# A transformer block with sliding attention and a token-mixing MLP: another hand-written issue order, with fillings in front of the first transposes

## The chip, the cores and the metric

The kernel runs on one core of one Trainium2 chip. The core has five engines that work side by side: PE (TensorE, matmuls), DVE (VectorE), ACT (ScalarE), POOL (GpSimd) and SP (SyncE, which here only issues DMAs). The metric is the device time of one launch in microseconds. Lower is better.

## The reference, cut

```python
mod = (silu(c) @ w_mod).reshape(1, 6, 1, 512)            # c: 1 x 512, w_mod: 512 x 3072
sa, ca, ga, sb, cb, gb = (mod[:, i] for i in range(6))
h = layernorm(x) * (1 + ca) + sa                          # x: 1 x 2048 x 512, bf16
x = x + ga * A(h)
h = layernorm(x) * (1 + cb) + sb
x = x + gb * B(h)
# A: qkv = h @ wqkv (512 x 1536); 32 heads of 16; each token attends to itself and the 7 tokens
#    at distances 2, 4, ..., 14 before it (softmax over 8); then @ wo (512 x 512)
# B: h = layernorm(h); u = gelu(w1^T h + b1) (w1: 2048 x 1792, over the tokens);
#    y = w2^T u + b2 (w2: 1792 x 2048)
```

A mixes neighbouring tokens. B mixes all tokens: every column of `w1` needs all 2048 rows of h.

## The kernel before, in words

**Tiles and chunks.** The 2048 tokens are 16 tiles of 128. They go through A in five chunks (numbered 0 to 4) of 2, 4, 4, 4 and 2 tiles, which begin at tiles 0, 2, 6, 10 and 14. In names a single digit after the kind of step is a chunk, and where tiles are meant the number runs from 0 to 15.

**First norm and transposition.** For each tile `ln1s` takes the statistics (on DVE one instruction; on ACT two passes with accumulation), `ln1v` gathers them, and `rstd1_`, `rste1_` and `nb1_` give one over the deviation and the shift for a chunk. `n1_` normalizes a tile. Chunks 0 and 1 are transposed on PE (`tr`) and copied out of PSUM with a scaling by `a1col`, which is 1 + ca as a column (`hT0_0` to `hT1_3`). Chunks 2 to 4 are transposed by DMAs that SP issues (`xt6` to `xt15`); for them `wqkv` itself is scaled by `a1col` (`wsc{t}_{kt}`; t is 0 for queries, 1 for keys, 2 for values). `a1col` comes from `modcols1`, 16 matmuls of one column of silu(c) with a part of `w_mod`. silu(c) comes from `cps`, a matmul on the loaded c (`ld_c`), an exponential on ACT and three instructions on DVE.

**Attention.** `qkv{chunk}_{t}{j}` are the products with `wqkv`, `ev...` the evictions that follow them (ACT or DVE). `qk` is a large elementwise product of queries and shifted keys on DVE; `red` sums it over a head's 16 numbers with matmuls on PE. `max`, `sub`, `exp`, `esum`, `rcp`, `rcq` and `smB` are the softmax. `a2_{chunk}_{0..3}` are four DMAs that spread the probabilities over the partitions, and `vd{chunk}_{0..3}` four DMAs that make shifted copies of the values (pool `vd`, five places). `pv` is the large product of both on DVE; it needs all four `a2_` of its chunk and its own `vd`. `pvacc` sums it on PE, `oev` evicts, `wo{tile}` multiplies by `wo` and adds the residual (with one matmul by the identity where ACT evicts, in the eviction where DVE does: `x1_{tile}`). `wo` has been scaled by ga (`woq_s`), which with the other rows of the modulation comes from `modrow`, `mrows` and the small loads `ld_row0` to `ld_row3`.

**Second and third norm, MLP.** `ln2*`, `n2_`, `aff`, `afb`, `ln3*` and `h3_` give h of B. `mlp1_{sweep}_{column}_{tile}` are partial products of the first MLP matrix over the tiles that are ready, in three sweeps; `park` and `padd` keep and add the partial sums in SBUF, `gelu` closes a column. `mlp2_{tile}`, `fin` and `st_out` are the second matrix, its bias and residual, and the stores.

**What sets the order.** All of the above is built as a graph of named steps. A table of names, `ORDER` (lines 180 to 235), gives the order in which they are issued, and nothing else plans: `schedule()` (line 87) walks the table, gives each step that needs one the place of its pool that came free first (6 PSUM banks `ps`, 4 product buffers `big`, 5 `vd`), and each engine runs its own steps in that order. A suffix chooses another of a step's forms: `:a` ACT, `:d` DVE, `:p` POOL, `:s` leaves it out, and `:q` splits each matmul into four strips of 32 output columns:

```python
def mm(out, lhsT, rhs, **kw):
    if not G.quad:
        return nc.tensor.matmul(out, lhsT=lhsT, rhs=rhs, **kw)
    for j in range(0, P, 32):
        nc.tensor.matmul(out[j:j + 32], lhsT=lhsT[:, j:j + 32], rhs=rhs, tile_position=(0, j), **kw)
```

Matmuls of `red`, `pvacc` and `modrow` have the strip form always. So the table says how often PE changes between the full form and the strip form.

**Fillings.** `WARM` gives the number of matmuls (512 columns of the identity, result not used) in the steps `warm0` to `warm7`. Before, it is `(12, 2, 2, 2, 2, 2, 2, 2)`. `warm0` is made to follow `cps` and to lie ahead of `modcols1` by a key (`wmA1`, lines 538, 553 and 556); `warm2` to `warm7` carry `:s` in the table, and `warm1` stands at its end.

All instructions are issued through one wrapper (`_EngProxy`), so every row of the profile says line 131; the steps are told apart by what they read and write: `xx` is x, `h` the normalized tiles, `hT` their transposes, `wst` a ring of weight places, `q_sb`, `k_f`, `v_sb` queries, keys and values, `lsb` the probabilities, `a2sb` the spread ones, `vD` the shifted values, `big` the products, `psS` and `psL` PSUM, `gT` the rows of the MLP.

Of the kernel before, what the change touches and what calls it, by code (L numbers as in the profile page):

```python
# [42 lines left out]
class _Graph:  # L43
# [7 lines left out]
    def add(self, eng, dur, fn, **kw):  # L51
        return self.add_any([(eng, dur, fn)], **kw)
# [138 lines left out]
nb1_3 a2_0_0 ln1s15:a a2_0_2 qkv2_00 qk1_2 qkv2_10 n1_13:p red1_0 ev2_00 red1_1 ev2_10 red1_2 red1_3 ln1v15 a2_0_1
ev1_23 qkv2_13:q qk2_0 ev1_21 max1 modrow qkv1_20:q sub1:q ln1s14:a a2_0_3 pv0_0 wsc2_1:a halo_v1:a qkv1_22:q mrows
vd0_3 vd0_1 vd0_2 ld_wo1 ev2_13 pv0_3 pvacc0_0 n1_10 exp1 ev1_20 ld_row0 qkv2_02:q pv0_1 pv0_2 warm3:s ld_wo2 esum1:q
rcp1 ev1_22 rcq1 smB1 qkv2_03 ev2_03 pvacc0_1 pvacc0_2 xt10 wsc2_0:a pvacc0_3 ev2_02 oev0_2 qkv2_01:q vd1_3 qkv2_12
oev0_0 ev2_01 ln1v14 qkv2_11 ev2_12 rstd1_4 qkv2_23:q n1_11 vd1_1 n1_12 a2_1_2 qkv2_22:q a2_1_3 qk2_3 woq_s rste1_4
wo1:q wo0:q ev2_11 a2_1_0 a2_1_1 vd1_2 x1_1 red2_0 qk2_2 nb1_4 qk2_1 ev2_22 qkv2_20 x1_0 ev2_23 ln2m0 biascols pv1_3
n1_14 xt13 xt12 ln2q0 ln2q1 n1_15 qkv2_21 red2_1 red2_2 ln2w0 red2_3 xt11 rstd2_0 pv1_1 ev2_21 rste2_0 qkv3_10:q
ev3_10 qkv3_02:q ev3_02 qkv3_00:q ev2_20 ev3_00 nb2_0 n2_1 n2_0 qkv3_11 max2 qkv3_01 ev3_01 sub2 pvacc1_1 oev1_1
halo_v2 ld_row2 vd1_0 pvacc1_3 pv1_2 qkv3_12:q ld_row1 exp2 aff0 ev3_12 qkv3_13:q halo_v3:a ev3_11 pv1_0 esum2
pvacc1_2 rcp2 oev1_3 oev1_2 afb0 pvacc1_0 oev1_0 rcq2 xt14 ld_w1_0_0 ld_w1_0_512 vd2_2 qkv3_03:q qk3_1 smB2 ln3s0:a  # L200
# [10 lines left out]
mlp1_0_7_0:q pv3_2 pvacc3_0 mlp1_0_5_2:q oev3_0 esum4:q nb2_6 n2_7 mlp1_0_6_2:q warm7:s rcp4 pv3_1 n2_6 park0_5 pv3_3
n2_9 pvacc3_2 n2_8 aff6 oev3_2 mlp1_0_7_2:q rcq4 pvacc3_1 oev3_1 mlp1_0_8_2:q smB4 ld_w1_0_1152 mlp1_0_10_0:q
ld_w1_0_1408 pvacc3_3 vd4_2 mlp1_0_10_2 vd4_0 warm2:s park0_6 oev3_3 wo11 afb6 x1_11:d a2_4_3 ln3s8 ln3v8 ln3s9:a wo10
wo13 ln3s6 vd4_1 ln3v9 ln3v6 ln3s7 wo12 x1_10 ln2m10 ln3v7 mlp1_0_9_0 ln2q11 x1_12:d mlp1_0_9_2 ln2q10 a2_4_0 ln2w10
rstd3_6 rste3_6 nb3_6 a2_4_2 h3_6:d h3_7:d mlp1_0_12_0 mlp1_0_12_2 h3_8:d rstd2_10 h3_9 mlp1_0_7_6 mlp1_0_8_6 ln2q12
# [23 lines left out]
def kernel(  # L239
# [72 lines left out]
    mask = T([32, NW, PAD], BF, "mask")  # L312
# [716 lines left out]
```

## Time and profile before

| | |
|---|---|
| runs | 198.03, 198.26, 198.43 us; median 198.26 |
| span of the profiled execution | 196.8 us, first to last instruction |
| own time of that execution | not recorded beside the span; the median lies 1.46 us above it |
| PE busy | 185.2 us (94%) |
| DVE busy | 156.6 us (80%) |
| ACT busy | 124.9 us (63%) |
| POOL busy | 19.9 us (10%) |
| DMA queue of SP | 34.05 MB, 63.2% of the time of 16 engines |

A row of the timeline is: start in us from the first instruction, duration, engine, line, operation, tile out <- tiles in, shape, and in brackets how long the engine had waited and for whom. Rows of equal instructions in a row are put together as xN, and the duration is then that of the whole run. PEld is the loading of weights into PE, which runs beside its matmuls; a `q` behind an engine (SPq, ACTq) is its issue of a DMA. In a table of windows stand the stretch, its length, and the busy time of each engine in it with the number of its instructions, then the clock that PE was granted (1.00 is full), the busy share of the DMA engines and GB/s. In a table of groups stand the count, the busy time in us, the mean of one in ns, and the idle time of the engine just before, with its releaser. A row of DMA issues has the count, the size of one and the median time from issue to landing.

### The profile page before, as it was taken

To read this page: it belongs to the slowest core of one execution; us is meant where nothing else is said; L and a number is where in the kernel's file an instruction comes from. 1 tells how busy PE (TensorE), PEld (TensorE's weight loads), DVE (VectorE), ACT (ScalarE), POOL (GpSimd) and SP (SyncE) were. 2 spreads that over 40 slices of the span, in tenths; PEclk is the share of its full clock that TensorE was granted. 3 is DMA by queue.
4 is the path that set the end of the run, shared out by engine and by line. 5 is a ranking of instruction groups with operands and counts; after the bars stand their busy time and mean duration, and the time that the engine had idled before them with its cause. 6 is when DMAs were issued, how large, how long until landed. Compare 5 with 4: busy or idle time off the path is not lost.

```text
span 196.8 us, 4628 instructions
## 1 busy us (share of the span) xinstructions
PE 185.2 (94%) x1850; PEld 95.5 (48%) x1867; DVE 156.6 (80%) x244; ACT 124.9 (63%) x293; POOL 19.9 (10%) x38
## 2 busy tenths in 40 slices
PE   0699999999999999899999999999999999999994
PEld 0369554654444467244544454444444444444453
DVE  2888999999999999999999999965841633453664
ACT  6877999998999999999797889812760000000000
POOL 5123006320000005030000031200000000000000
PEclk9999999999999999999999999999999999999999
DMA  5998478778899732969674768888939293001112
GB/s 169 312 366 248 115 165 256 235 216 238 165 193 317 252 131 80 312 167 249 199 200 136 159 176 180 197 250 170 336 65 309 82 257 102 30 27 53 53 53 82
DMA packets 55369, 35.95 MB, mean 183 GB/s; under 512 B 24628, under 2 KB 52788, under 8 KB 55348
## 3 DMA queue, kind: packets, MB, share of 16 engines
q1 hardware_dynamic: 53468, 34.05, 63.2%
q10 hardware_dynamic: 1880, 1.61, 2.5%
q8 instruction: 14, 0.23, 0.5%
q14 instruction: 7, 0.06, 0.1%
HBM read 22.03 MB, written 2.10 MB: 123 GB/s over the span
## 4 chain that ended last, share of the span: by engine, by line
PE 73%; DVE 13%; ACT 5%; issue 3%; DMA 2%; SPq 1%; POOL 0%; DVEq 0%; ACTq 0%
PE psS L131 71%; DVE big L131 9%; DVE h L131 2%; PE psL L131 2%; ACT junk L131 1%; SPq L131 1%; DMA vD<-v_sb 1%; ACT xx L131 1%; DMA xx<-in_A_x_dram 1%; DVE m L131 1%; ACT o_sb L131 1%; ACT lsb L131 0%; DVE mv L131 0%; POOL h L131 0%; ACT v_sb L131 0%
## 5 line engine op out<-in xcount | busy, mean ns | idle before, releaser
L131 PEld LDWEIGHTS <-wst 128*128 128x128 bf16 (+1 forms) x566 | 35.5, 100 | 31.9 <-issue 1.3
L131 PE MATMUL psS<-h,wst 128*32 128x512 bf16 (+1 forms) x400 | 50.5, 379 | 0.4 <-issue 0.3
L131 DVE TENSOR_TENSOR big<-q_sb,k_f 128x4096 bf16<-128x4096 bf16 (+1 forms) x20 | 36.4, 1857 | 0.5 <-ACT k_f L131 0.5
L131 DVE TENSOR_TENSOR big<-a2sb,vD 128x4096 bf16<-128x4096 bf16 (+1 forms) x20 | 36.6, 1858 | 0.0
L131 DVE SCALAR_TENSOR_TENSOR h<-psS,bcol,rows_bc 128x512 f32<-128x512 f32 (+2 forms) x18 | 12.4, 690 | 24.2 <-PE psS L131 24.0
L131 PE MATMUL psS<-hT,w_qkv 128*32 128x512 bf16 (+3 forms) x414 | 28.7, 337 | 0.8 <-ACT v_sb L131 0.4
L131 PEld LDWEIGHTS <-w_qkv 128*32 128x32 bf16 (+1 forms) x462 | 19.9, 108 | 16.4 <-issue 2.7
L131 PE MATMUL psS<-gT,big 128*128 128x512 bf16 x109 | 24.3, 379 | 0.2
L131 POOL TENSOR_SCALAR h<-xx,rs,nb 128x512 bf16<-128x512 bf16 x6 | 10.6, 1777 | 84.2 <-DVE nb L131 84.2
L131 PEld LDWEIGHTS <-big 128*128 128x128 bf16 x144 | 12.0, 98 | 13.7 <-issue 0.5
L131 ACT ACTIVATE junk<-xx 128x512 bf16<-128x512 bf16 x28 | 17.7, 631 | 1.3 <-DVE xx L131 0.3
L131 ACT ACTIVATE h<-xx,nb,rs 128x512 bf16<-128x512 bf16 x22 | 17.2, 818 | 0.4 <-DVE nb L131 0.4
L131 PE MATMUL psS<-woq,o_sb 128*32 128x512 bf16 (+1 forms) x123 | 15.8, 380 | 0.4 <-ACT o_sb L131 0.4
L131 ACT ACTIVATE gT<-psS,bcol 128x512 bf16<-128x512 f32 x14 | 8.8, 686 | 10.6 <-DVE psS L131 10.6
L131 DVE TENSOR_TENSOR psS<-psS,gT 128x512 f32<-128x512 f32 x14 | 9.2, 695 | 6.3 <-PE psS L131 6.3
L131 DVE TENSOR_TENSOR h<-h,xx 128x512 bf16<-128x512 f32 (+2 forms) x18 | 11.4, 633 | 0.7
L131 ACT ACTIVATE q_sb<-psS,qvb 128x512 bf16<-128x512 f32 (+1 forms) x20 | 11.6, 603 | 0.3 <-PE psS L131 0.2
L131 PEld LDWEIGHTS <-group 128*32 128x32 bf16 x288 | 7.0, 96 | 9.8 <-issue 4.0
L131 PE MATMUL psS<-hT,wst 128*128 128x256 bf16 (+2 forms) x74 | 11.3, 333 | 0.1
L131 ACT ACTIVATE v_sb<-psS,qvb 128x512 bf16<-128x512 f32 (+1 forms) x20 | 11.2, 607 | 0.0
L131 DVE TENSOR_TENSOR h<-h,rows_bc 128x1024 bf16<-128x1024 bf16 (+2 forms) x14 | 10.5, 759 | 0.0
L131 ACT ACTIVATE k_f<-psS 128x512 bf16<-128x512 f32 x16 | 9.7, 606 | 1.1 <-PE psS L131 1.1
(90 smaller groups left out, 223.3 us busy)
## 6 DMA issues: line engine op xcount, KB each, us to landing
vD<-v_sb SPq DMA_DIRECT2D x12, 524.5 KB, 4.8
big<-in_B_w_dram SPq DMA_DIRECT2D x4, 896.0 KB, 7.5
vD<-v_sb SPq DMA_DIRECT2D x8, 268.5 KB, 3.1
wst<-in_B_w_dram SPq DMA_DIRECT2D x3, 640.0 KB, 5.4
xx<-in_A_x_dram SPq DMA_DIRECT2D x7, 256.0 KB, 5.6
wst<-in_B_w_dram SPq DMA_DIRECT2D x2, 800.0 KB, 4.7
gT<-in_w_mod_dram SPq DMA_DIRECT2D x3, 512.0 KB, 5.4
wst<-in_B_w_dram SPq DMA_DIRECT2D x2, 768.0 KB, 5.6
```

What stands on the lines that cost most here:

```text
L131: r = fn(*a, **k)
```

## The change

Five edits. All but two are in the table.

1. `WARM` becomes `(2, 8, 1, 3, 8, 5, 2, 1)`, and all eight steps are now issued. On PE: `warm0` to `warm3` (14 matmuls), `cps`, `warm4` and `warm5` (13), the transposes of chunk 0, `warm6` (2), `modcols1`. `warm7` (1) stands in front of `wo7`. The key `wmA1` is gone.
2. The load of c (`ld_c`, issued by ACT) moves from the front of the table to behind `rste1_0` on ACT; `ident` is the first work of POOL, and the zero halos (`halo0`) come behind the constants.
3. SP's queue has another order. At the front: tiles 0 and 1 of x, then the pairs 4-5, 2-3, 8-9, 6-7, both parts of `w_mod`, the query weights (`ld_wqkv0`), **the pair 10-11 of x (chunk 3's first)**, the key weights (`ld_wqkv1`), the value weights, the pairs 12-13 and 14-15. Later: the four `a2_0` are preceded by `vd0_3` alone; `ld_wo2`, `ld_wo3`, `xt10`, `ld_wo0`, `ld_wo1`, `ld_b1`, `ld_row0`, `vd1_1`, `xt11`, `a2_1_3`, `xt12`, `a2_1_1`, `a2_1_2`, `a2_1_0`, `xt13`, `ld_row2`, `vd1_0`, `vd1_3`, `vd1_2`. Before, in that place: three of the four `ld_wo` earlier, `vd1_3`, `vd1_1`, the four `a2_1`, `vd1_2`, `xt13`, `xt12`, `xt11`, `ld_row2`, `vd1_0`.
4. Other engines. From ACT to DVE 17 steps: the evictions `ev0_00`, `ev0_02` and `ev1_22`, `n1_1`, `n1_3`, `n1_8`, `n2_14`, `h3_5`, `h3_9`, `x1_10`, and statistics of seven tiles. From ACT to POOL 11: `n1_7`, `n1_9`, `n1_14`, `n2_3`, `h3_10`, `h3_15`, `halo_v4`, and the weight scalings `wsc1_0`, `wsc1_1`, `wsc2_0`, `wsc2_2`. From DVE to ACT 20: `hT0_2`, `hT1_0`, `hT1_2`, `n1_2`, `n1_4`, `n1_5`, `wsc0_0`, five `h3_` and eight statistics. From POOL to ACT five (`n1_13`, `n2_5`, `n2_15`, `wsc1_2`, `halo_v2`), from POOL to DVE three (`n1_0`, `wsc0_2`, `h3_11`), from DVE to POOL one (`h3_12`). `nb1_0` is left out (its tiles are normalized on DVE), `nb3_12` and `nb3_14` are issued. Of the stores eight go from ACT to SP and two from SP to ACT.
5. Fewer steps carry `:q`: PE's matmul and weight-load instructions fall from 3736 to 3496. The order of steps on every engine is another, the kinds of work and their sum the same; in the MLP other columns go into the first sweeps' early and late pieces, and the last pieces of the last tile end in the order 0, 1, 2 (before 0, 2, 1).

```diff
-halo0 ident ld_c act_table cps silu_exp ld_x1 ld_x0 ln1s0 ln1v0 ln1s1:a ln1v1 rstd1_0 rste1_0 ld_x_2_8 ld_x_1_2 nb1_0
-consts ln1s9 silu_dve n1_1 n1_0:p tr0_0 ln1s8 ld_x_1_4 ln1s4:a ld_x_2_6 ln1s3:a warm0 ln1s5 ln1s7 ld_wmod1 ln1v5
-ld_wmod0 modcols1 modcols0 ln1v9 ln1v8 ln1v4 ln1s2 ln1v2 ld_wqkv0 ln1v7 ln1v3 ln1s6 ln1v6 rstd1_1 rste1_1 nb1_1 n1_4:d
-rstd1_2 rste1_2 n1_2:d n1_5:d nb1_2 ld_wqkv1 n1_3 n1_7 n1_6:d a1col hT0_2:d n1_9 tr1_2 tr1_0 hT1_1 wsc0_1:p hT0_1:d
-sab hT0_0:d ld_x_3_12 hT0_3:d hT1_3:d qvb0 qvb_cp0 qkv0_00 warm6:s wsc1_3:a hT1_2:d qkv0_02 ev0_00 ld_wqkv2 qkv0_10
-qkv0_12 ld_b2 ev0_10 ld_x_4_14 wsc1_2:p qkv0_20 wsc0_0 qvb1 ld_x_3_10 wsc0_3:p hT1_0:d ev0_02 wsc2_2:a ln1s13 ln1s12
...
+ld_x0 ident act_table ln1s0 consts ld_x1 ln1s1 ln1v1 ln1v0 rstd1_0 warm0 rste1_0 ld_x_1_4 ln1s5 ld_c warm1 ld_x_1_2
+nb1_0:s ld_x_2_8 warm2 ln1s4 ln1v5 ln1s3 n1_0:d ln1v3 n1_1:d ln1s2:a ln1v4 ln1v2 ld_x_2_6 ln1s8 warm3 cps rstd1_1
+rste1_1 silu_exp nb1_1 ln1s6:a warm4 ld_wmod1 warm5 ln1s9 halo0 silu_dve ln1v9 tr0_0 n1_4 warm6 ln1s7 ld_wmod0
+modcols1 ld_wqkv0 a1col n1_2 wsc0_1:p n1_5 wsc0_3:p ln1v6 modcols0 ln1v8 ln1v7 ld_x_3_10 rstd1_2 rste1_2 hT0_3:d hT0_2
+ld_wqkv1 n1_3:d hT0_1:d hT0_0:d tr1_0 nb1_2 tr1_2 sab hT1_0 ln1s10 hT1_2 ld_wqkv2 ld_x_3_12 qvb0 ln1s11:a n1_9:p
+hT1_3:d wsc0_0:a qkv0_00 hT1_1 qkv0_02 qvb_cp0 qkv0_10 n1_8:d qkv0_12 wsc0_2 ld_x_4_14 qkv0_22 ld_wmod2 ev0_10 ev0_12
+ev0_02:d qkv0_20 ld_wmod3 n1_6:d xt6 qkv1_11 wsc2_3:a n1_7:p qvb1 ld_wmod4 ev0_00:d qk0_0 qk0_1 red0_0 qkv1_01:q
...
+ev2_01 n1_11 ld_b1 ev2_11 pvacc0_1 ev2_10 n1_12 qkv2_03:q ev2_03 pvacc0_3 ld_row0 n1_13 vd1_1 oev0_2 smB1 qkv2_00
+oev0_0 xt11 a2_1_3 qkv2_20 xt12 qkv2_22 qk2_2 a2_1_1 ev2_00 qkv2_13 ev2_13 qk2_1 woq_s qk2_0 qk2_3 wo1 x1_1 ln2q1
+ev2_21 wo0 red2_0 a2_1_2 x1_0 ln2m0 ln2q0 qkv2_23:q a2_1_0 red2_1 ev2_23 ev2_20 pv1_1 halo_v2:a xt13 ld_row2 vd1_0
+ln2w0 rstd2_0 rste2_0 red2_2 red2_3 ev2_22 qkv3_03 max2 ev3_03 qkv3_11 qkv3_10 vd1_3 sub2 qkv3_01 vd1_2 ev3_10 nb2_0
...
-    WARM=(12, 2, 2, 2, 2, 2, 2, 2),
+    WARM=(2, 8, 1, 3, 8, 5, 2, 1),
...
-        if w_ == 0:
-            f_warm0, s_w0 = f_warm, s_w
-            continue
...
-    add("pe", 0.216 * WARM[0], f_warm0, after=[G.ops[-1]], alloc=s_w0, frees=s_w0, writes=["wmA1"], name="warm0")
...
-    add("pe", 0.42, lambda: f_cols(1), reads=["sc", ("wmodA", 1), "wmA1"], writes=["wmA1"], alloc=s_m[1], name="modcols1")
+    add("pe", 0.42, lambda: f_cols(1), reads=["sc", ("wmodA", 1)], alloc=s_m[1], name="modcols1")
```

More of the change, by code (lines that the diff above doesn't have):

```diff
@@ L191 @@
[L191 to L200, printed above, removed]
@@ L211 @@
[L211 to L215, printed above, removed]
@@ new lines @@
+a2_0_3 rstd1_4 qk1_3 ev1_22:d rste1_4 nb1_4 halo_v1:a n1_14:p vd0_0 rstd1_3 vd0_2 vd0_1 rste1_3 red1_3 wsc1_2:a
+wsc1_3:a nb1_3 max1 pv0_3 qkv2_02 ev1_20 qkv2_01 ld_wo2 pv0_0 ld_wo3 n1_10 n1_15 ev2_02 sub1 exp1 ev1_21 qkv2_12
+modrow ev2_12 pvacc0_0 mrows esum1:q qkv2_21:q pv0_2 pv0_1 rcp1 pvacc0_2 qkv2_11:q rcq1 xt10 ld_wo0 qkv2_10:q ld_wo1
+ev2_01 n1_11 ld_b1 ev2_11 pvacc0_1 ev2_10 n1_12 qkv2_03:q ev2_03 pvacc0_3 ld_row0 n1_13 vd1_1 oev0_2 smB1 qkv2_00
+oev0_0 xt11 a2_1_3 qkv2_20 xt12 qkv2_22 qk2_2 a2_1_1 ev2_00 qkv2_13 ev2_13 qk2_1 woq_s qk2_0 qk2_3 wo1 x1_1 ln2q1
@@ new lines @@
+pv3_3 park0_4 park0_5 n2_7 esum4:q ld_w1_0_1408 rcp4 n2_8 aff6 rcq4 park0_6 mlp1_0_10_0:q vd4_0 oev3_1 mlp1_0_9_0:q
+vd4_2 mlp1_0_9_2:q afb6 pvacc3_0 mlp1_0_10_2:q pvacc3_3 oev3_0 oev3_3 smB4 a2_4_0 ln3s7:a ln3s6 mlp1_0_8_2 a2_4_2 wo12
+a2_4_3 wo11 x1_12:d wo13 x1_11:d ln3s9 a2_4_1 vd4_3 wo10 ln3s8:a x1_10:d ln2m10 mlp1_0_11_0 mlp1_0_11_2 mlp1_0_12_0
+ln2q11 mlp1_0_12_2 ln2q10 ln3v7 ln3v9 ln3v6 ln3v8 x1_13:d ln2m12 mlp1_0_7_0 rstd3_6 rste3_6 mlp1_0_7_2 nb3_6 h3_7:d
+h3_8:d h3_6 ln2q12 ln2w10 h3_9:d mlp1_0_7_6 vd4_1 rstd2_10 rste2_10 ln2q13 mlp1_0_8_6 pv4_2 mlp1_0_9_6 nb2_10 pv4_1
```

70 lines of the change are left out of this document (36 added, 34 removed).

## The prediction

> **What bounds the kernel now.** I read the page first, then the busy time of four stretches, then the timeline of each engine around the places that the change touches.
>
> ```profile
> span 196.8 us, 4628 instructions
> PE 185.2 (94%) x1850; PEld 95.5 (48%) x1867; DVE 156.6 (80%) x244; ACT 124.9 (63%) x293; POOL 19.9 (10%) x38
> ```
>
> ```profile
> 12.33:42.00 29.67, 29.30 (x400) 19.49 (x405) 28.45 (x38) 27.46 (x60) 8.64 (x6) 1.00 0.73 206
> 42.00:102.00 60.00, 58.29 (x885) 29.96 (x887) 59.87 (x60) 57.25 (x140) 4.71 (x4) 1.00 0.78 211
> 102.00:126.00 24.00, 23.68 (x220) 11.04 (x219) 23.51 (x64) 20.39 (x58) 3.30 (x4) 1.00 0.73 185
> 126.00:191.00 65.00, 64.68 (x299) 29.65 (x304) 33.64 (x51) 10.78 (x16) 0.00 (x0) 1.00 0.50 139
> ```
>
> The columns after the length are PE, PEld, DVE, ACT and POOL. PE's 94% tempts one to call the kernel PE-bound and every filled PE gap a gain. The stretches say otherwise. From 42 to 102 DVE is busy 59.87 of 60.00 us, PE 58.29. From 126 on DVE is half idle and PE is full: 299 matmuls in 65 us, 0.217 us each. Where one bound hands over to the other is seen at 102:
>
> ```profile
> 97.35 4.49 DVE L131 TENSOR_TENSOR big<-a2sb,vD 128x4096 bf16<-128x4096 bf16 x2
> 101.89 0.62 PE L131 MATMUL psS<-big,group 128*32 128x512 bf16 x8
> ```
>
> DVE ends the last two value products of chunk 3 at 97.35 + 4.49 = 101.84, and PE starts their sum (pvacc3_3) at 101.89. PE stands there because DVE has just got there. All that follows (the rest of the first MLP matrix, then the second) is one queue of PE work of fixed length. So the time is: start of DVE's dense stretch, plus DVE's work up to pv3_3, plus PE's work behind it, plus the stores. What PE gains ahead of 102 is lost again in waits for DVE.
>
> **The lead-in.** DVE's dense stretch begins at 18.07, and these rows lead to it.
>
> ```profile
> 0.81 0.56 ACTq L131 DMA_DIRECT2D c_t<-in_c_dram  x1
> 1.25 0.29 POOL L131 TENSOR_SCALAR_AFFINE_SELECT ident<-ident 128x128 bf16<-128x128 bf16 x1
> 2.20 0.18 PE L131 MATMUL psS<-ident,c_t 4*128 4x4 bf16 x1 [2.20 <-DMA c_t<-in_c_dram]
> 3.73 1.02 SPq L131 DMA_DIRECT2D big<-in_w_mod_dram  x2
> 5.14 0.20 ACT L131 ACTIVATE rs<-lv 128x2 f32<-128x2 f32 x1
> 7.30 5.20 PE L131 MATMUL psS<-ident 128*128 128x512 bf16 x12
> 11.38 2.21 ACT L131 ACTIVATE h<-xx,nb,rs 128x512 bf16<-128x512 bf16 x3
> 12.33 0.94 PE L131 MATMUL psS<-sc,big 128*128 128x1 bf16 x32
> 12.90 0.16 DVE L131 TENSOR_SCALAR a1col<-psS 128x4 f32<-128x4 f32 x1 [0.59 <-PE psS L131]
> 13.13 1.05 PE L131 MATMUL psS<-ident,h 128*128 128x128 bf16 x16
> 14.22 0.69 ACT L131 ACTIVATE hT<-psS,a1col 128x512 bf16<-128x512 bf16 x1 [0.64 <-PE psS L131]
> 14.55 3.66 PE L131 MATMUL psS<-hT,wst 128*128 128x256 bf16 x32
> 17.38 0.60 ACT L131 ACTIVATE k_f<-psS 128x512 bf16<-128x512 f32 x1 [0.91 <-PE psS L131]
> 18.07 2.36 DVE L131 TENSOR_TENSOR big<-q_sb,k_f 128x2048 bf16<-128x2048 bf16 x2 [0.51 <-ACT k_f L131]
> ```
>
> The 12 fillings (warm0) take 5.20/12 = 0.433 us each, twice the 0.217 of later; the array had worked without a gap for at least 5.0 us (7.30 to 12.33) when the rate doubled. Before: modcols1 waits for the fillings until 12.33, a1col is there at 12.90, the key eviction ev0_10 at 17.38, qk0_1 at 18.07.
>
> After, PE has 14 fillings ahead of the matmul on c, 13 behind it, 8 transposes, 2 fillings, then modcols1. The identity is POOL's first work now (the zero halos come later): start about 1.5. 14 x 0.433 = 6.1, to 7.6. The load of c is moved behind ACT's rste1_0, which ends at 5.34; in the row it took 1.39 us from issue to use, so c is there at 6.7, under that cover. Over 5.0 us of gap-free work have passed, so I take the 13 at 0.217: 2.8, to 10.4; 8 transposes at half of the 1.05 us that 16 take: to 10.9; 2 fillings: modcols1 at 11.3, one microsecond earlier than before. Its weights were issued at 3.73; the six input loads ahead of them are the same bytes in another order.
>
> ```profile
> big<-in_w_mod_dram SPq DMA_DIRECT2D x2, 512.0 KB, 6.0
> L131 ACT ACTIVATE junk<-xx 128x512 bf16<-128x512 bf16 x28 | 17.7, 631 | 1.3 <-DVE xx L131 0.3 <-DMA xx<-in_A_x_dram 0.3
> L131 ACT ACTIVATION_READ_ACCUMULATOR junk<-xx 128x1 f32 x28 | 5.4, 193 | 0.0
> L131 DVE TENSOR_SCALAR h<-h,mv,rs 128x512 bf16<-128x512 bf16 x9 | 3.2, 404 | 0.0
> L131 DVE TENSOR_TENSOR gT<-psS,gT 128x512 bf16<-128x512 f32 x7 | 4.4, 682 | 0.3 <-PE psS L131 0.3
> ```
>
> They land at 9.7 (first row), in time. But the gain isn't handed on. Before, DVE had normalized chunk 1 when a1col came. After, n1_3 stands behind a1col on DVE (a1col 11.9, three short statistics, one hT0 of 0.3, n1_3 of 0.40), so it is ready at 13.0; the other three are on ACT in a run like that at 11.38. The transposes of chunk 1 start at 13.1, where before they start at 13.13. Behind them ACT has hT1_0, hT1_2, the two statistics passes of tile 11 (2 x (0.63 + 0.19), some 1.5 with overlap), wsc0_0 and hT1_1, then ev0_10: 13.1 + 0.6 for the first transposes, four steps of about 0.6 (0.69 less 0.09 overlap), 1.5: ev0_10 starts at 17.6 and ends at 18.25. PE has its keys ready earlier (qkv0_00 at 14.1, third product done by 16.9), so the pair of chunk 3 put ahead of the key weights costs nothing here: I cover it by this ACT run. If the key weights came over 1 us later than qkv0_10 wants them, that cover would be gone. So DVE starts at 18.3: **+0.2 us**. Bounds: -0.8 if the PE gain of 1.0 came through whole, +2.1 if all 27 fillings ran at 0.433 (2.8 us more, of which the 0.7 in front of n1_3 absorb some).
>
> The clock is where the Trainium skill can be weighed (TensorE: Matmul & The Clock Gate, Part 1). It says that the array starts at half clock, and that about 3.4 us of sustained activity, seen in a free-running window, release it. The trace's 5.0 us or more agree with such a window missed once. By that rule the fillings would speed up at 5 to 8 us, modcols1 would come at 10.9 to 11.9, and the sum below would move by -0.3 to +0.4.
>
> **DVE's work up to pv3_3.** Both kernels do 20 qk and 16 pv products there. After the change one eviction more is on DVE (ev1_22, as the 682 ns row), two more aggregations (0.1 each from start to start), and one normalization of h3 less (0.33): **+0.5 us**. The evictions ev0_00 and ev0_02 move to DVE ahead of 18.3 into its waits. Four weight scalings and five norms move to POOL:
>
> ```profile
> 5.64 0.77 POOL L131 TENSOR_SCALAR h<-xx,rs,nb 128x512 bf16<-128x512 bf16 x1 [2.11 <-DVE nb L131]
> 31.42 4.91 POOL L131 TENSOR_SCALAR h<-xx,rs,nb 128x512 bf16<-128x512 bf16 x1 [15.17 <-DVE nb L131]
> ```
>
> The same operation takes 0.77 us with DVE light and 4.91 beside dense products. Two of the scalings (wsc2_0, wsc1_1) fall behind 18 us and may end only at 26; their first reader qkv2_12 comes at 36. Cost 0; bound +0.8 for one such operation that holds DVE up.
>
> **PE ahead of 102.** Fewer matmuls are split in four column strips, so PE changes less often between full and strip form, 23 to 13 times before pvacc3_3. The price:
>
> ```profile
> 48.75 0.60 PE L131 MATMUL psL<-big,group 128*32 128x512 bf16 x8
> 49.29 1.05 PE L131 MATMUL psS<-hT,w_qkv 128*128 128x512 bf16 x3
> 68.09 0.60 PE L131 MATMUL psL<-big,group 128*32 128x512 bf16 x8
> 68.52 2.77 PE L131 MATMUL psS<-hT,w_qkv 128*32 128x512 bf16 x64
> ```
>
> The same eight matmuls take 0.54 with a change of form behind them, 0.43 without: 0.11 each, 1.1 us for ten. All of it lies in PE's waits for DVE, as does warm7 (0.2). I count 0; bound -1.1. Behind 102 the count of changes is three in both, and wo10 loses its matmul with the identity: **-0.2 us**.
>
> **SP's queue.** This is where I look for what is late next. For chunk 1 SP now issues: two output-weight loads, xt10, two more, b1, row0, vd1_1, xt11, the first a2_1, xt12, three a2_1, xt13, row2, vd1_0.
>
> ```profile
> 38.59 2.37 SPq L131 DMA_TRANSPOSE hT<-h  x1
> 46.55 4.58 SPq L131 DMA_TRANSPOSE hT<-h  x3
> 51.81 0.60 SPq L131 DMA_DIRECT2D vD<-v_sb  x1
> 58.71 2.28 DVE L131 TENSOR_TENSOR big<-a2sb,vD 128x4096 bf16<-128x4096 bf16 x1
> a2sb<-lsb SPq DMA_DIRECT2D x12, 64.0 KB, 3.3
> vD<-v_sb SPq DMA_DIRECT2D x8, 268.5 KB, 3.1
> vD<-v_sb SPq DMA_DIRECT2D x12, 524.5 KB, 4.8
> ```
>
> Before, vd1_0 is issued at 51.81 and read last of its four, at 58.71: 6.9 us of cover. After, it is read second (pv1_0). With 0.65 for a plain issue, 2.4 for the transpose behind plain ones and 1.55 for the others, SP reaches the last a2_1 at about 48.4 and vd1_0 at 51.4. DVE reaches pv1_1 at about 51 and pv1_0 at about 54.5. Landing after 3.3 and 4.8 us gives 51.7 and 56.2: DVE would wait 0.7 and then 1.0 more. With the 3.1 of the smaller transfer vd1_0 is there at 54.5, and with faster transposes nothing waits. Ends 0 and 1.8; I take **+0.7**, between, since the transfer's queue is lighter there than in the median. Nothing behind it absorbs this, as DVE is dense.
>
> Sum: +0.2 + 0.5 - 0.2 + 0.7 = +1.2; rounded down for the slack that I rounded off, +1.0. The profiled execution has a span of 196.8, 1.46 under the median 198.26 of the three runs; I carry that difference over: 197.8 and **199.2 us**.
>
> **Rivals.** (A) Faster: lead-in first. If ACT's run behind the transposes is hidden (by reading ahead in the gaps of 10 to 13 us), DVE starts 0.8 earlier, and if SP is in time: -0.8 + 0.5 - 0.2 = -0.5, 197.8; with the ten form changes counting in part, 197.3. For it: PE reaches modcols1 1 us sooner. Against it: n1_3 behind a1col. (B) No difference: +0.2 + 0.5 - 0.2 with a start 0.3 earlier, SP in time: 198.3 to 198.6. (C) SP's queue as the new bound, at its worst: 1.8 instead of 0.7: 200.3. It decides from the point where vd1_0 is issued later than 4.8 us before pv1_0. (D) The fillings stay slow and delay modcols1: up to +2.1, 200.4 to 201. (E) POOL's lock: the Trainium skill (SBUF — State Buffer, "Who interferes with whom") says that GpSimd and a two-input DVE operation exclude each other, and whichever starts first blocks the other. The trace shows only POOL losing (4.91), with the products beside it at their usual 2.28. As a mechanism of this kernel: three POOL operations that catch a short DVE gap, 0.77 each, would add 2.3 to DVE: 201.5.
>
> **How the numbers follow.** The forecast's family (DVE late by 0.5 to 1.2) has 0.40, C 0.12, D 0.05, E 0.03: slower 0.60. B has 0.16, A 0.24. The range 197.4 to 201.0 takes in A and C and most of D; the slower cases alone give 198.7 to 201.0. 0.2% (0.4 us) is about what a measurement of this kernel can tell from no change. DVE's bound works against every PE gain, hence the lean to slower; A keeps a quarter because the lead-in terms are differences of long chains.
>
> **What would show it.** Right: the first qk at 18.0 to 18.6; pvacc3_3 right behind DVE's last pv of chunk 3, near 103; a DVE gap released by a vD or a2sb transfer at 50 to 56; PE waits for DVE ahead of 102 grown by about the 1 to 2 us that it gained. Wrong: the first qk before 17.5; or DVE idle ahead of 102 elsewhere; or PE full ahead of 102, with the time set by PE's own queue.

## The result and the profile after

The changed kernel takes 205.81 us (median of four runs, 205.29 to 206.45) where the kernel before took 198.19 beside it: ratio 1.0376, 95% interval 1.0335 to 1.0416. The forecast was 199.2 us with a range of 197.4 to 201.0. The direction was right, the size was not: 7.6 us instead of 1.0.

The page of the kernel after, its head, and the lines of its chain that ended last:

```profile
span 203.6 us, 4407 instructions
...
PE 191.5 (94%) x1747; PEld 96.7 (47%) x1747; DVE 158.4 (78%) x245; ACT 124.8 (61%) x290; POOL 16.4 (8%) x42
...
PE 52%; DVE 20%; ACT 10%; DMA 8%; issue 7%; SPq 1%; DVEq 0%; ACTq 0%
```

The profiled execution took 205.33 us with this span of 203.6, 6.8 us more than the 196.8 of before; that is the difference to be explained. The busy shares tell nothing: PE is at 94% in both. The chain does. In the kernel before PE had 73% of it and DMAs 2%; now PE has 52%, DMAs 8%. Followed in order of time, its first 24 us name the transfer (start, length, what):

```profile
4.88 0.01 ACT rs L131
4.89 4.68 DMA c_t<-in_c_dram
...
9.62 6.04 PE psS L131 x40
...
15.69 0.16 DVE a1col L131
```

The timeline of the kernel after shows what stands around it, in rows that answer to those of the lead-in before:

```profile
1.43 5.67 PE L131 MATMUL psS<-ident 128*128 128x512 bf16 x14 [1.43 <-POOL epscol L131]
...
4.89 0.55 ACTq L131 DMA_DIRECT2D c_t<-in_c_dram  x1
...
9.62 0.17 PE L131 MATMUL psS<-ident,c_t 4*128 4x4 bf16 x1 [2.52 <-DMA c_t<-in_c_dram]
9.72 4.67 PE L131 MATMUL psS<-ident 128*128 128x512 bf16 x13
...
15.11 0.94 PE L131 MATMUL psS<-sc,big 128*128 128x1 bf16 x32
...
22.43 2.36 DVE L131 TENSOR_TENSOR big<-q_sb,k_f 128x2048 bf16<-128x2048 bf16 x2
```

c is 1 KB. Issued at 0.81 in the kernel before, it was there when PE wanted it at 2.20. Issued at 4.89, behind nine loads of 128 to 512 KB on SP's queue, it is there at 9.57. PE has done its 14 fillings at 7.10 and stands for 2.52 us. Then the 13 fillings behind take 4.67 us, 0.36 each, where the forecast had 0.217. Windows of the kernel after say why (stretch, length, PE busy, granted clock, DMA share, GB/s):

```profile
0.00:9.50 9.50, 5.67 (x14) 1.00 0.75 238
9.50:10.00 0.50, 0.38 (x2) 0.88 1.08 381
10.00:13.00 3.00, 3.00 (x9) 0.50 1.08 373
13.00:13.50 0.50, 0.50 (x3) 0.71 1.11 358
13.50:15.00 1.50, 1.50 (x15) 1.00 1.10 350
```

From 9.88 (0.88 is a quarter of that half microsecond at 0.50) to 13.29 the granted clock is half: 3.41 us, in which matmuls take 0.433. They take as much at the start, where the column shows 1.00 all the same, so it marks this second slow stretch and not the first. The first 14 fillings took 5.67 us, 0.39 less than 14 x 0.433, so I estimate that their rate doubled near the end, between 6.5 and 6.7 us. So the fillings ahead of the matmul on c worked until PE ran at its full rate, the wait for c lost that rate again, and modcols1 comes at 15.11 instead of 11.3. The Trainium skill (TensorE: Matmul & The Clock Gate, Part 1) describes windows of about 3.4 us, after an idle one of which the array is back at half clock. The length agrees with the 3.41, but the 3.41 us ahead of 9.88 were not wholly idle here: PE worked some 0.9 of them, with a gap of 2.52 us.

Behind the first qk, DVE shows one wait, and the end of its dense stretch follows (timeline of the kernel after, DVE and PE):

```profile
42.75 3.50 DVE L131 TENSOR_TENSOR big<-a2sb,vD 128x2048 bf16<-128x2048 bf16 x3 [1.56 <-DMA vD<-v_sb]
...
101.49 6.69 DVE L131 TENSOR_TENSOR big<-a2sb,vD 128x4096 bf16<-128x4096 bf16 x3
108.24 0.61 PE L131 MATMUL psS<-big,group 128*32 128x512 bf16 x8
```

DVE's last value product of chunk 3 ends at 101.49 + 6.69 = 108.18 and PE goes on at 108.24: the hand-over is as before, 6.3 us later. So the 6.8 us are: first qk 4.36 later (22.43 against 18.07); between it and the last pv of chunk 3 85.75 against 83.77, that is 1.98, with 1.56 in the one wait for vD and 0.42 in DVE's work; from PE's sum behind it to the end 95.4 against 94.9, 0.5.

### The profile page after: what moved, and what is told of

Read it like the earlier page. It is cut to its first block, busy times and chain, and to the rows that moved or that the text cites. A ratio compares the mean times of both kernels' runs of the same rounds, so it can differ in the third digit from the quotient of the medians.

```text
span 203.6 us, 4407 instructions
## 1 busy us (share of the span) xinstructions
PE 191.5 (94%) x1747; PEld 96.7 (47%) x1747; DVE 158.4 (78%) x245; ACT 124.8 (61%) x290; POOL 16.4 (8%) x42
## 4 chain that ended last, share of the span: by engine, by line
PE 52%; DVE 20%; ACT 10%; DMA 8%; issue 7%; SPq 1%; DVEq 0%; ACTq 0%
PE psS L131 52%; DVE big L131 10%; ACT junk L131 3%; DMA wst<-in_B_w_dram 3%; DMA c_t<-in_c_dram 2%; DMA vD<-v_sb 2%; DVE h L131 2%; ACT h L131 2%; ACT xx L131 2%; DVE st L131 2%; DVE m L131 2%; DVE mv L131 1%; SPq L131 1%; DMA xx<-in_A_x_dram 1%; ACT lsb L131 1%
## 5 line engine op out<-in xcount | busy, mean ns | idle before, releaser
L131 PEld LDWEIGHTS <-wst 128*128 128x128 bf16 (+1 forms) x524 | 35.5, 100 | 33.5 <-issue 1.8
L131 PE MATMUL psS<-h,wst 128*128 128x512 bf16 (+1 forms) x338 | 50.6, 379 | 0.2
L131 DVE TENSOR_TENSOR big<-a2sb,vD 128x4096 bf16<-128x4096 bf16 (+1 forms) x20 | 36.5, 1860 | 1.6 <-DMA vD<-v_sb 1.6
L131 DVE TENSOR_TENSOR big<-q_sb,k_f 128x4096 bf16<-128x4096 bf16 (+1 forms) x20 | 36.5, 1858 | 0.1
L131 PE MATMUL psS<-hT,w_qkv 128*32 128x256 bf16 (+2 forms) x360 | 29.1, 323 | 0.0
L131 PE MATMUL psS<-gT,big 128*128 128x512 bf16 x112 | 24.8, 379 | 0.0
L131 ACT ACTIVATE h<-xx,nb,rs 128x512 bf16<-128x512 bf16 x20 | 15.6, 810 | 0.7 <-DVE nb L131 0.4
L131 PE MATMUL psS<-woq,o_sb 128*128 128x512 bf16 x64 | 15.9, 379 | 0.0
L131 PE MATMUL psS<-ident 128*128 128x512 bf16 x30 | 11.3, 547 | 1.4 <-POOL epscol L131 1.4
L131 POOL TENSOR_SCALAR h<-xx,rs,nb 128x512 bf16<-128x512 bf16 x6 | 5.3, 889 | 89.5 <-DVE nb L131 88.9
L131 PE MATMUL psS<-big,group 128*32 128x512 bf16 (+1 forms) x160 | 9.6, 338 | 3.0 <-DVE big L131 2.3
L131 PEld LDWEIGHTS <-ident 128*32 128x32 bf16 (+1 forms) x153 | 7.2, 104 | 10.6 <-issue 6.9
L131 PE MATMUL psS<-hT,wst 128*32 128x512 bf16 (+2 forms) x100 | 11.4, 345 | 0.0
## 6 DMA issues: line engine op xcount, KB each, us to landing
vD<-v_sb SPq DMA_DIRECT2D x8, 268.5 KB, 4.8
```

The source lines that it names most:

```text
L131: r = fn(*a, **k)
```

## The experiments

Each kernel was timed against the kernel before on the same chip; medians of the kernel before beside them were 198.35 to 198.7.

**c first** (in the kernel after):

```diff
-... rstd1_0 warm0 rste1_0 ld_x_1_4 ln1s5 ld_c warm1 ...
+ld_c ld_x0 ident act_table ... rste1_0 ld_x_1_4 ln1s5 warm1 ...
```

> The kernel after, with one step moved: the load of c is again ACT's first issue (before ld_x0 in the table). Theory L (the late load of c): c lands near 2 us instead of 9.46, cps follows the 14 fillings at 7.1 without the gap of 2.5 us, the 13 fillings behind it run at 0.216 instead of 0.433, modcols1 comes at 11.1 instead of 15.1, the first qk at 18.4 instead of 22.4: 4.0 us less than the kernel after, 201.3 us. Rival W (the fillings are too many wherever they stand): modcols1 stays behind 13, first qk behind 20, 203.5 or more. Rival N (lead-in hidden, the loss lies behind it): 205 to 206.

Measured: 201.65 us, ratio 1.0142 (1.0121 to 1.0163). Its PE timeline:

```profile
1.43 5.54 PE L131 MATMUL psS<-ident 128*128 128x512 bf16 x14 [1.43 <-POOL epscol L131]
6.90 0.17 PE L131 MATMUL psS<-ident,c_t 4*128 4x4 bf16 x1
7.01 2.98 PE L131 MATMUL psS<-ident 128*128 128x512 bf16 x13
...
10.70 0.94 PE L131 MATMUL psS<-sc,big 128*128 128x1 bf16 x32
```

No gap, 13 fillings in 2.98 us, modcols1 at 10.70, first qk at 17.87. One small load's place is worth 4.2 us of the 7.6 (4.6 by the two ratios). Theory L holds, and some 3 us over the kernel before are left to explain.

**c late in the kernel before**:

```diff
-halo0 ident ld_c act_table cps silu_exp ld_x1 ... rste1_0 ... silu_dve n1_1 n1_0:p tr0_0 ...
+halo0 ident act_table ld_x1 ... rste1_0 ld_c ... n1_1 n1_0:p tr0_0 cps ... ln1s3:a silu_exp warm0 ... ln1v5 silu_dve ...
```

> The kernel before with the load of c behind rste1_0 on ACT (as in the kernel after); cps goes behind tr0_0 on PE, its exponential behind the statistics of tiles 3 and 4 on ACT, its three DVE instructions behind ln1v5, so that only c's lateness acts; warm0 still follows cps. Theory L: c lands near 9.5, warm0 starts there, 12 x 0.433 to 14.9, modcols1 at 14.7 to 15.0 instead of 12.33, first qk at 20.5 instead of 18.07: 2.4 us slower than the kernel before, 200.7 us. Rival (c comes in time from ACT's queue, and what is late in the kernel after comes from its other order): modcols1 at 12.3 to 12.6, 198 to 198.6 us.

Measured: 201.9 us, ratio 1.0143 (1.0108 to 1.0178); c was used at 10.30, and the fillings behind it took 0.40 each (4.81 for 12), PE having run only eight transposes before; modcols1 came at 15.05, the first qk at 20.80, 2.7 later. The same move costs 3.2 us in the old table too, where 2.4 were expected.

**Bridge** (c late as in the kernel after, PE kept busy until it comes):

```diff
-    WARM=(2, 8, 1, 3, 8, 5, 2, 1),
+    WARM=(2, 8, 1, 15, 2, 2, 2, 1),
```

> The kernel after with c as late as there, but the fillings spread otherwise: 26 ahead of cps instead of 14, 4 behind it instead of 13 (WARM=(2,8,1,15,2,2,2,1)), so that PE works without a gap until c is there. It separates c's lateness from the loss of the clock in the gap. Theory L with the clock: granted at 6.5, the rest of the front at 0.216 to 9.6, cps 9.65, modcols1 near 11.5, first qk near 18.8, 201.7 us. If only c's lateness counted and the clock not, the fillings ahead of cps would end near 12.7 and the 4 behind would go on at 0.433: modcols1 at 15 or later, 205 us or more.

Measured: 203.08 us, ratio 1.0245 (1.019 to 1.0301). On its PE timeline the 26 fillings ended at 8.67, the gap was 1.16 us, and no window at 0.50 followed:

```profile
1.43 7.24 PE L131 MATMUL psS<-ident 128*128 128x512 bf16 x26 [1.43 <-POOL epscol L131]
9.83 0.17 PE L131 MATMUL psS<-ident,c_t 4*128 4x4 bf16 x1 [1.16 <-DMA c_t<-in_c_dram]
9.94 1.04 PE L131 MATMUL psS<-ident 128*128 128x512 bf16 x4
...
11.69 0.94 PE L131 MATMUL psS<-sc,big 128*128 128x1 bf16 x32
```

modcols1 comes at 11.69 as expected; the first qk at 19.83, not 18.8: the late exponential of c on ACT and its three instructions on DVE stand ahead of statistics and norms on both, and these came later too. So of the 4.56 us between the kernel after (22.43) and c first (17.87), 2.6 go away with the gap and its slow fillings, and 2.0 stay with c's lateness.

One of the four executions of this kernel took 205.42 us, 2.4 more than the other three, with a mean granted clock of 0.992, that of the kernel after; the others show 1.0. There is no trace of it, but 3.41 us at 0.50 in a span of 203.7 make just this 0.992. So the same gap seems to have lost the clock in one execution and not in three, at a price near the 2.6 us.

**No fillings** (c first):

```diff
-... warm0 ... warm1 ... warm2 ... warm3 cps ... warm4 ... warm5 ... tr0_0 n1_4 warm6 ...
+... warm0:s ... warm1:s ... warm2:s ... warm3:s cps ... warm4:s ... warm5:s ... tr0_0 n1_4 warm6:s ...
```

> The kernel after with c first and without any filling ahead of modcols1 (warm0 to warm6 left out). It prices the fillings. Theory: the weights of modcols1 land at 10.3, so it comes at 10.4 with or without them; without, the array is at half rate until 3.4 to 6.8 us of work have passed, that is to 14 or 17, and the first qk comes at 18.3 to 20.5 instead of 17.9: 202 to 204 us against 201.65. Rival (the fillings are worth nothing, since the first qk waits for ACT's evictions): first qk at 17.9, 201.5 to 201.8.

Measured: 201.14 us, ratio 1.0144 over the kernel before in its runs (1.0112 to 1.0177), against 201.65 (201.12 to 201.94) with 29 fillings: no slower. The rival forecast no gain from the fillings, which is the result, but not for the reason that it gave. PE's row of the first products is slow, and yet nothing is lost:

```profile
13.82 5.71 PE L131 MATMUL psS<-hT,wst 128*128 128x256 bf16 x32
```

These 32 matmuls take 3.66 with the clock granted; the first qk came at 19.70, 1.8 later than with the fillings. But two losses of the run with c first are not there. One is DVE's wait at pv0_0, 1.45 us; why, the runs on vd0 below tell. The other stands in DVE's rows with c first:

```profile
17.87 2.71 DVE L131 TENSOR_TENSOR big<-q_sb,k_f 128x2048 bf16<-128x2048 bf16 x2
20.50 0.56 DVE L131 SCALAR_TENSOR_TENSOR mv<-mv,st 128x1 f32<-128x1 f32 x1
```

Without fillings the same two rows take 2.36 and 0.21. With c first a weight scaling on POOL runs beside them, from 18.35 for 2.71 us, where the scaling ahead of it took 0.69; without fillings POOL has ended at 18.82, before the products begin. So 1.83 us of a later start stand against 1.45 and 0.70, and the last pv of chunk 3 ends at 104.06 against 104.21. The fillings did bring DVE's start forward; a transfer and POOL took it back.

**The halves of the table.** New lead-in (c first) with the old rest, and old lead-in with the new rest:

```diff
+# f1: after's ORDER up to ev0_00:d (ld_c first), then before's ORDER without the steps already done
+# f2: before's ORDER up to qkv0_22, then after's ORDER without the steps already done
```

> A hybrid: the lead-in of the kernel after up to the first qk, with the load of c first, and behind it the table of the kernel before (the statistics of tiles 12 and 13 stand behind qk0_3 on DVE, 1.4 us there, and that of tile 10, 0.7 us, is already done). It prices the new lead-in alone. Theory H (the lead-in's gain is not handed on: modcols1 at 10.7 against 12.33, the first qk at 17.9 against 18.07): DVE starts 0.2 earlier, has 0.6 more to do, 199.0 to 199.5 us where the kernel before takes 198.7 beside it. Rival A (the gain of 1.6 us comes through): 197.4 to 198.0.

Measured: 199.41 us, ratio 1.0045 (1.0021 to 1.0068); modcols1 at 10.28, first qk at 17.92, last pv of chunk 3 at 102.44. The gain of 2.05 us at modcols1 is 0.15 at the first qk, as theory H has it.

> The other hybrid: the lead-in of the kernel before up to the first qk (12 fillings, c first), and behind it the table of the kernel after (warm7 skipped; on DVE ln1s10, n1_8 and wsc0_2 stand behind qk0_3, 1.5 us). It prices everything behind the lead-in. If the wait at pv0_0 (1.5), the DVE work (1.1) and the later last store (0.4) are properties of the rest: first qk at 18.1, 201.5 to 202.5 us, 3 us over the kernel before. If they were consequences of the new lead-in: 199 us or less.

Measured: 201.85 us, ratio 1.016 (1.0128 to 1.0191). The rest costs 3.2 us without the new lead-in, so its loss is no consequence of that; but the parts were not those expected. DVE did not wait for vD. It waited 1.4 for ACT's statistics of tile 11 right behind the first qk, which is a seam of this hybrid (they are part of the other lead-in), so that some 1.8 us belong to the rest itself (waits of DVE, this kernel: engine, line, waited for, sum, times, longest):

```profile
DVE mv L131 <- ACT junk L131: 1.4, 1, 1.4
```

**The place of vd0.** One of them ahead of the `a2_0`, or all four (with ev0_22 earlier on ACT), both with c first:

```diff
-... smB0 vd0_3 qkv1_22:q ln1v10 ev1_13 a2_0_1 ... n1_14:p vd0_0 rstd1_3 vd0_2 vd0_1 ...
+... smB0 vd0_3 vd0_0 qkv1_22:q ln1v10 ev1_13 a2_0_1 ... n1_14:p rstd1_3 vd0_2 vd0_1 ...          # one
+... ev0_20 ev0_22 ev1_02 xt7 ... xt8 vd0_3 vd0_0 vd0_2 vd0_1 esum0 ... smB0 qkv1_22:q ...         # all four
```

> As the run with c first, and vd0_0 moved on SP's queue from behind the four a2_0 to right behind vd0_3. Theory Q (DVE's 1.56 us at pv0_0 come from the place of vd0_0 in SP's queue): that wait goes, a2_0 come 0.65 later, which DVE sees as at most 0.4: 199.9 to 200.3 us, 1.0 to 1.4 below the run with c first. Rival F (the wait is the 16 KB code fetch that took 1.57 us on one DMA engine at 39.5 and struck whatever transfer was there): the wait moves to another transfer or vanishes in the run with c first already, and the two runs agree within 0.4 us.

Measured: 200.82 us, ratio 1.0094 (1.0075 to 1.0112), 0.8 below c first, between the two theories. Its trace can't tell the share of the wait: it is of an execution of 204.19 us, in which PE was granted 0.50 of its clock from 14.5 to 17.9. There the wait stands split over two of the four products, 0.48 and 0.37, and 0.62 more are waited for a vD of chunk 2.

> The kernel after with c first, and all four vd0 on SP's queue ahead of the a2_0, right behind xt8, where SP is idle; for that ev0_22 goes behind ev0_20 on ACT. Theory Q: the 1.45 us that DVE waited at pv0_0 are gone, no new wait: 200.1 to 200.4 us, against 201.65 with c first alone. Rival: ev0_22 ahead of the evictions of chunk 1 delays qk1_0 or qk1_2 by its 0.7, and half of it is lost: 200.8 to 201.

Measured: 200.61 us, ratio 1.0106 (1.0072 to 1.0139), some 0.7 below c first by the ratios (the two were timed on different chips), between theory and rival. The four products of chunk 0 run without a wait; 0.42 of the 1.45 us came back as a wait for a vD of chunk 2:

```profile
36.48 4.62 DVE L131 TENSOR_TENSOR big<-a2sb,vD 128x2048 bf16<-128x2048 bf16 x4
```

What lengthened the transfer is in the DMA rows over the time of vd0_0, first of the kernel after (38.3 to 42.8), then of the kernel without fillings (35.5 to 38.1):

```profile
DMA  4930015820099989998998890101010000499899
...
q8 instruction: 1, 0.02, 2.2%
...
vD<-v_sb SPq DMA_DIRECT2D x3, 268.5 KB, 4.8
```

```profile
q1 hardware_dynamic: 784, 0.55, 64.5%
...
vD<-v_sb SPq DMA_DIRECT2D x3, 268.5 KB, 2.5
```

In the first a block of 16 KB of instructions is fetched in one packet; its 2.2% of 16 engines in 4.5 us are 1.6 us of one engine. The row `DMA` gives the busy tenths of the 16 engines in 40 slices: from 41.0 to 42.1 they are all but idle, ahead of the end of the wait at 42.75. I read this as one engine that, late by the fetch, still works off its share; then the three vD take 4.8 us instead of 2.5. In the second no instruction queue is listed. The same holds elsewhere: with c first (34.4 to 38.8) there is one such fetch and 4.7 us, in the bridge one and 4.5, with the old lead-in (36.5 to 39.1) none and 2.7. SP issues vd0_0 behind the a2_0 in all five, so the place alone does not cost; it leaves no cover, and whether a fetch falls there seems to depend on the instructions ahead, the fillings among them. That the fetch is the cause, and that fewer fillings shift it, is read from these traces and was not tried by itself.

**DVE's added work back to ACT**, on top of the last:

```diff
-... ev1_22:d ... ln1s15 ... ln3s2 ...
+... ev1_22 ... ln1s15:a ... ln3s2:a ...
```

> As the last run, and three steps go back from DVE to ACT: the eviction ev1_22 (0.66 on DVE) and the statistics of tile 15 (first norm) and tile 2 (third norm), 0.60 each. If DVE is the bound up to pv3_3 and ACT has room, 1.2 to 1.9 us go: 198.3 to 199.0 us. Rival: ACT, 95 to 97% busy in these stretches, becomes late and DVE waits for it: 199.8 to 200.4, no gain.

Measured: 202.77 us, ratio 1.0214 (1.0184 to 1.0245), 2.2 slower. 1.9 us of DVE's work went, and yet its stretch to the last pv grew from 85.13 to 88.05, by waits, most of them for ACT (waits of DVE in this kernel):

```profile
DVE mv L131 <- ACT junk L131: 1.3, 2, 1.1
...
DVE nb L131 <- ACT rs L131: 0.7, 3, 0.4
DVE big L131 <- ACT k_f L131: 0.7, 1, 0.7
DVE lsb L131 <- ACT rb L131: 0.7, 1, 0.7
```

The rival holds: ACT is as full as DVE there. DVE's busy time did not fall either (84.53 against 84.58), because small steps grew: those that gather statistics took 2.6 us instead of 1.2, 0.8 of it in two that ran beside POOL's scalings. So that these moves to DVE were a gain by themselves is likely, and its size is not known.

**Can the lead-in's gain be handed on?** First n1_3 alone, with c first:

```diff
-... ld_wqkv1 n1_3:d hT0_1:d ...
+... ln1s9 n1_3:d halo0 silu_dve ...
```

> The kernel after with c first, and n1_3 on DVE ahead of a1col (behind ln1s9) instead of behind it; nothing else. If n1_3 is what held the transposes of chunk 1 and, through them, the first qk: tr1 ends at 12.5 instead of 13.35, qkv0_00 starts 0.4 earlier, first qk at 17.4 to 17.5, 201.2 us (201.65 without). Rival (the keys' eviction is held by ACT's run of two hT1, statistics and a scaling): first qk stays at 17.8 to 17.9, 201.6 us.

Measured: 201.55 us, ratio 1.0147 (1.0124 to 1.0171). The transposes ended at 12.53 as expected, but the first qk stayed at 17.84: PE then waited 0.91 for sab on DVE. Naming n1_3 as what holds the gain was too narrow.

Then an order for the whole lead-in, on the hybrid with the old rest:

```diff
+# key weights ahead of x_3_10 on SP; n1_3 ahead of a1col; hT0_0..3 on DVE right behind a1col
+# PE: tr1 qkv0_00 qvb0 qkv0_10 qkv0_02 qkv0_12; ev0_02 on ACT; wsc0_0, wsc1_1, wsc2_2 on POOL
```

> A try at a version that hands the lead-in's gain on, built on the hybrid with the new lead-in and the old rest: n1_3 ahead of a1col on DVE, the four hT0 on DVE right behind a1col, the key weights ahead of the pair 10-11 of x on SP, PE's order tr1, qkv0_00, qvb0, qkv0_10, qkv0_02, qkv0_12, ev0_10 on ACT ahead of the statistics of tile 11, ev0_02 back on ACT, and three more weight scalings on POOL. Theory H (what held the gain was the order behind modcols1): modcols1 at 10.5, qkv0_00 at 12.7 instead of 14.0, first qk near 16.0 instead of 17.9; DVE has some 1.2 us more to do behind it than in the kernel before: 197.4 to 198.2 us, 0.5 to 1.2 below the kernel before. Rival (ACT, with the evictions of chunk 1 behind, or the landing of weights sets DVE's pace as soon as it starts earlier): first qk near 16, but DVE waits by 1 to 2 us before 30: 198.5 to 199.5.

Measured: 199.7 us, ratio 1.0069 (1.0047 to 1.0092). The first qk came at 16.30, 1.8 us before that of the kernel before, and the last pv of chunk 3 at 102.57, 0.7 after. POOL's rows of this kernel, and DVE's:

```profile
16.77 2.71 POOL L131 TENSOR_SCALAR w_qkv<-wst,a1col 128x512 bf16<-128x512 bf16 x1
19.45 1.65 POOL L131 TENSOR_SCALAR w_qkv<-h,a1col 128x512 bf16<-128x512 bf16 x1
21.09 1.65 POOL L131 TENSOR_SCALAR w_qkv<-wst,a1col 128x512 bf16<-128x512 bf16 x1
```

```profile
16.30 4.25 DVE L131 TENSOR_TENSOR big<-q_sb,k_f 128x2048 bf16<-128x2048 bf16 x3 [0.40 <-ACT k_f L131]
...
20.56 1.62 DVE L131 TENSOR_TENSOR big<-q_sb,k_f 128x2048 bf16<-128x2048 bf16 x1
```

One such product takes 1.22 alone; here it takes 1.62, and three take 4.25 instead of 3.50. So POOL does not only lose beside DVE.

```diff
+# wsc0_0, wsc1_1, wsc1_2, wsc2_2 on ACT; hT1_3 ahead of qkv0_00's evictions; ln1s10 ahead of the first qk
```

> The try before (first qk at 16.3, but 199.7 us) with what ate its gain taken out. There the four qk0 took 1.49 to 1.63 instead of 1.13 beside three weight scalings on POOL (16.8 to 22.7), 1.2 us in all, and the statistics of tile 10 had moved behind them, 0.6. Now the scalings wsc0_0, wsc1_1, wsc1_2 and wsc2_2 are on ACT (in its waits at 14.4, 19.9 to 21.4 and 22.0), hT1_3 is in DVE's wait at 13.4, and ln1s10 is ahead of the first qk. Theory P (POOL's work beside the products cost DVE 0.4 each): the four qk0 at 1.13 to 1.2, last pv of chunk 3 at 100.8 instead of 102.6, 197.8 to 198.1 us, 0.4 to 0.8 below the kernel before. Rival (DVE then waits for ACT's evictions of chunk 1): no change, 199 to 199.7.

Measured: 198.99 us, ratio 1.0036 (1.001 to 1.0061). Timeline of DVE in this kernel:

```profile
16.58 3.50 DVE L131 TENSOR_TENSOR big<-q_sb,k_f 128x2048 bf16<-128x2048 bf16 x3 [0.20 <-ACT k_f L131]
20.74 0.16 DVE L131 COPY qvb<-psS 128x4 f32<-128x4 f32 x1 [0.66 <-PE psS L131]
20.82 1.23 DVE L131 TENSOR_TENSOR big<-q_sb,k_f 128x2048 bf16<-128x2048 bf16 x1
```

With POOL idle the three take 3.50 and the fourth 1.23, as theory P has it for POOL. The sum still misses 1.0 us (last pv at 101.86, not 100.8), of which 0.66 is a new wait for PE.

```diff
-... qkv1_03:q qvb_cp1 qk0_3 ...
+... qkv1_03:q qk0_3 qvb_cp1 ...
```

> The last try (first qk at 16.6, last pv of chunk 3 at 101.9, as late as in the kernel before) with one step moved: qvb_cp1, on which DVE waited 0.67 us for PE at 20.1, goes behind qk0_3, which does not need it. Theory D (DVE is dense from the first qk on, so each wait or instruction taken from it comes through to the end): the wait goes, last pv of chunk 3 at 101.2, 198.3 us where 198.99 was, within 0.2 of the kernel before. Rival (something else, PE's products or ACT's evictions of chunk 1, is 0.7 late as well and takes the wait's place): last pv at 101.8, 198.9 us.

Measured: 198.64 us, ratio 1.0004 (0.9986 to 1.0021): no difference from the kernel before. The wait went there and came back two steps on:

```profile
16.08 4.63 DVE L131 TENSOR_TENSOR big<-q_sb,k_f 128x2048 bf16<-128x2048 bf16 x4
...
23.14 0.69 DVE L131 TENSOR_REDUCE m<-psL 128x64 bf16<-128x512 f32 x1 [0.69 <-PE psL L131]
```

The first qk is 2.0 us earlier than in the kernel before, the last pv at 101.64 against 101.84. Of the 1.8 lost between, 0.7 is the wait for PE's sums ahead of max0; 1.5 are the statistics of tiles 12 and 13 with their aggregations, which the kernel before had done in the lead-in while DVE waited, against 0.7 for those of tile 10, now done ahead; the remaining 0.3 are small. The rival holds. No order tried here beats the kernel before.

## Why the prediction was wrong, and where it was right

**The step that failed** is "in the row it took 1.39 us from issue to use, so c is there at 6.7, under that cover". The row was of a load issued first into idle DMA engines; the moved load was issued at 4.89 into a queue of loads, and took 4.68. The nearest rows for a load of that time were those of the x pairs and of w_mod, 5.6 and 6.0 us to landing, and they stood on the page. With them c would have come at 10.5 or 10.9, and the sum would have been some 3 us higher even with a granted clock. The range missed for the same reason: this cost had no bound from the other side. Of the 6.6 us between 199.2 and 205.81, 4.1 are the first qk (22.43 for 18.3); DVE's wait has 0.9 (1.56 for 0.7), the work behind 102 has 0.7 (+0.5 for -0.2), the time outside the span 0.75 (2.21 for the 1.46 carried over) and the rounding 0.2. That c came over ACT's queue did not help it; the Trainium skill (DMA: Bandwidth & Descriptors, "Issuing engines are not separate DMA queues") says that transfers from all engines interleave on the same 16 DMA engines, and the two times, 4.68 and 1.39 for the same 1 KB, agree.

**Fillings.** "So I take the 13 at 0.217" followed from there being no gap. With c first it was right: 2.98 for 13 (0.229 each), modcols1 at 10.70 where 11.3 stood. With c late they took 4.67. Rival D named slow fillings, at +2.1 and with a chance of 0.05; its price left out that what makes them slow also makes them start late. Against the first qk forecast at 18.3, the kernel after is 4.1 later, and c first takes 4.56 away.

**The gain of the lead-in.** "The gain isn't handed on" was right in result (c first: 17.87, 0.2 before the old 18.07; I had 0.2 after), and rival A was wrong. The reason given, n1_3, was one link of several: without it the chain is held by sab, then by the keys' eviction, and with an order of its own for all of these by PE and by the statistics that found no other place. That the pair of chunk 3 ahead of the key weights costs nothing was read from traces only: in the run with c first PE takes up the keys' product right behind the queries'.

**DVE's work** was forecast at +0.5 and measured at +0.42. **SP's queue** was the right suspect with a fair size (0.7, up to 1.8, where its parts 0.7 and 1.0 make 1.7; measured 1.56) and the wrong place: I looked at vd1_0, which came in time, and not at vd0_0, which had also been moved behind the transfers it once preceded, and I had no term for an instruction fetch. That the size fits is luck. **Behind 102** I had -0.2; PE's work from pvacc3_3 to its last piece took 92.0 against 91.9, and the end behind that was 0.4 later, which stays open: with the same stores the time from the last one's issue to the end lay between 2.3 and 2.7 us in different kernels. **Ahead of 102** the fewer changes of form showed no effect on the end; PE waited longer for DVE instead, 1.17 us before a sum of chunk 2 where the kernel before has 0.5. That was forecast.

**POOL.** Rival E had the mechanism and the wrong price: in the run where three scalings lay beside the first products, these took 0.4 more each, not 0.77. The Trainium skill (SBUF — State Buffer, "Who interferes with whom") says that an operation of GpSimd and a two-input one of DVE exclude each other; the 1.62 against 1.22 agrees. In the kernel after POOL had done its six scalings by 22.3, ahead of the late first qk, so there it cost nothing; with c first the last of them met the first products and cost DVE 0.7.

## What to carry to other kernels

A load that is moved is priced by the transfers in flight where it is moved to, not by its old row, however small it is: look for the rows issued at that time. One dependence in the middle of a run of fillings can cost both its own wait and the clock behind it, as c did here. What a filling is worth is read at the engine that sets the end, and here they brought the first product 1.8 us forward and the end not at all, because a transfer and POOL stood in the way behind it. When two or three engines are full at once, time won at the start is lost to the next of them within a few microseconds, and work taken off the fullest engine may cost more on the next.

## What was not expected of the hardware

A gap of 2.52 us on PE was followed by a window of 3.41 us at half of the granted clock. The length of a gap alone does not decide: after one of 1.16 us three executions of four kept the clock, and in the execution of 204.19 us a window of the same length, at 0.50 from 14.52 to 17.93, followed gaps of 0.62, 0.84 and 0.76 us. In the 3.41 us ahead of the two windows that were traced PE was idle for 2.5 and 1.6 us; that what counts is the work in a window of this length is a guess from two cases. Transfers of 268.5 KB took 4.5 to 5.5 us in four traces in which a fetch of 16 KB of instructions met them (the kernel after, c first, the bridge, n1_3 alone), and 2.5 and 2.7 in two in which none did. Weight scalings on POOL beside DVE's products took 1.65 to 2.71 us instead of 0.7 and made these 1.62 instead of 1.22; on DVE itself such a scaling takes 0.34, less than what one on POOL cost DVE there.
